# Units 8 to 31 of an attention kernel: two engines' queues in the order in which the program is written, with the pieces of a unit regrouped

## The chip, the cores and the metric

The kernel runs on one core of a Trainium2 chip. A core has a matrix engine (TensorE, PE in the rows; its weight loads are listed apart as PEld), a vector engine (VectorE, DVE), a scalar engine (ScalarE, ACT), a general engine (GpSimd, POOL) and a queue for transfers (SyncE, SP). Each engine works off its own queue in order and waits for others at semaphores. The metric is the device time of one execution in microseconds (us).

## The reference

Attention over 4 batches, 8 heads, 576 positions and 64 dimensions a head, followed by a two-layer network with a squared ReLU. To the scores of each head a bias is added that depends on the query's and the key's position alone; a small network of 32 hidden values makes it:

```
scores = scale * np.matmul(q, k.transpose(0, 1, 3, 2))
x = (psi_rel / psi_i)[..., None]
bias = np.maximum(x @ w1 + b1, 0.0) @ w2
scores = scores + bias.transpose(2, 0, 1)[None, :, :, :]
attn = softmax(scores)
out = np.matmul(attn, v)
h = np.maximum(out_as_tokens @ w_in, 0.0)
result = (h * h) @ w_out
```

## The kernel before

**Units.** A unit is one pair of heads of one batch and one chunk of 128 query positions (chunk 4 is the tail with 64 positions, in which the two heads share one tile). Units 0 to 39 (`NA` = 40) treat batches 0 and 1, eight units a chunk (`AB * HP` = 8), the tail's chunk first. While the eight units of one chunk run, the bias of the next chunk is made in 18 blocks of 32 key positions; units 0 to 31 make bias, units 32 to 39 have none left to make. Units from 40 on, and the two-layer network behind them, belong to other parts of the program, which the change does not touch.

**What a unit does.** The names are those of the rows:

- `sp` (L421): four score products into a PSUM tile of four banks, of which there is one.
- `t` (L431): VectorE adds the bias to a head's scores and finds the largest; twice a unit, once a head. `negm` is the largest.
- `p` (L436): ScalarE's exponential, twice a unit. The two are called the first and the second exponential here.
- `pp`, `pa` (L524, L516): TensorE transposes the probabilities of the unit two before (`TL` = 2): `pp` is four pieces of one head, so there are two of them a unit, the first and the second `pp`; `pa` is the last piece of both heads. ScalarE copies each to `pt` (L827).
- `bb` (L381): the masked products of a block, sixteen matrix products on a 0/1 mask that VectorE makes (`mask`, L371). ScalarE scales one half of a block (`bt`, L386); behind that, VectorE multiplies the other half (`bt`, L387); GpSimd adds them into the bias (`area`, L395). The mask tiles are three (`MB` = 3).
- `px` (L542): the products with the values, of a unit whose `pt` is there; VectorE copies the result (`xT`, L555; in the first eight units ScalarE does, L553).

**Blocks of a unit.** `BO` gives the number of blocks that are done by the end of each of the eight units of a chunk; from it units 8 to 15 have 1, 2, 3, 2, 3, 2, 3 and 2 blocks, as have 16 to 23; units 24 to 31 have 1, 2, 3, 2, 3, 2, 3 and 0.

**Banks.** The results `pp`, `pa`, `bb` and `px` go to four PSUM banks which one pool hands out in turn (`bank`, tag `aux`, four buffers). A result that comes fourth after another takes that one's bank, and TensorE's first product into it waits until the earlier result has been read out.

**Order.** The loop is written unit by unit: scores, exponentials, bias blocks, transposes, values. For units 0 to 39 a scheduler sorts each engine's queue by a simulated time of readiness; `keep_in_program_order` pins single instructions. Behind unit 39 the blocks `with tc.manual_schedule()` keep every queue in the order of the program text.

Of the kernel before, what the change touches and what calls it, by code (L numbers as in the profile page):

```python
# [22 lines left out]
HP = H // 2  # L23
# [4 lines left out]
AB = 2  # L28
NF = DFF // 128
NIC = 5  # L30
TAIL = 4
NJB = S // 32
# [6 lines left out]
BO, B1 = (3, 5, 8, 10, 13, 15, 18, 20), (12, 3, 8)  # L39
# [23 lines left out]
MB = 3  # L63
# [5 lines left out]
TL = 2  # L69
# [8 lines left out]
def attention_then_relu2_mlp(ctx: ExitStack, tc: tile.TileContext, q, k, v, cols, w_in, w_out, psi, xmat, dist, out):  # L78
# [64 lines left out]
    NA = len(units)  # L143
# [215 lines left out]
    def bias_mask(ic, jb):  # L359
        m = prep.tile([128, 8, 128], F16, name="mask", tag="mask", bufs=MB)  # L360
        if ic < TAIL:
            base = sdist[:, 128 * ic + 548 - 32 * jb:]
            win = bass.AP(tensor=base.tensor, offset=base.offset, ap=[base.ap[0], [4, 8], [1, 128]])
            th = theta[:, 128 * ic:128 * ic + 128].unsqueeze(1).to_broadcast([128, 8, 128])
            out = m
        else:
            base = sdist[:, 128 * ic + 548 - 32 * jb - HALF:]
            win = bass.AP(tensor=base.tensor, offset=base.offset, ap=[base.ap[0], [4, 8], [HALF, 2], [1, 64]])
            th = theta[:, 512:].unsqueeze(1).unsqueeze(1).to_broadcast([128, 8, 2, 64])
            out = m.rearrange("p g (x i) -> p g x i", x=2)  # L370
        DVE.tensor_tensor(out=out, in0=win, in1=th, op=ALU.is_ge)  # L371
        mask_t[ic, jb] = m

    def bias_sum(ic, jb):
        m = mask_t.pop((ic, jb))
        bb = bank("bb")
        t = prep.tile([128, H, 32], F32, name="bt1", tag="bt1", bufs=BB)
        s = prep.tile([128, H, 32], F32, name="bt2", tag="bt2", bufs=BB)
        for r in range(8):
            for n in range(2):  # L380
                PE.matmul(bb[:, 64 * (7 - r):64 * (8 - r)], lhsT=m[:, r], rhs=wmov[:, n], start=(n == 0), stop=(n == 1))  # L381
        xv = xc_t[ic][:, 32 * jb:32 * jb + 32].rearrange("p (g j) -> p g j", j=4).unsqueeze(1)
        bv = bb.rearrange("p (g a h j) -> p a h g j", g=8, a=2, h=H)
        tv = t.rearrange("p h (g j) -> p h g j", j=4)
        sv = s.rearrange("p h (g j) -> p h g j", j=4)
        ACT.activation(out=sv, in_=bv[:, 1], func=AF.Identity, scale=bscale)  # L386
        DVE.tensor_tensor(out=tv, in0=bv[:, 0], in1=xv.to_broadcast([128, H, 8, 4]), op=ALU.mult)  # L387
        if ic == TAIL:
            (POOL if jb < 7 else DVE).tensor_tensor(out=tail_sum[:, :, 32 * jb:32 * jb + 32], in0=t, in1=s, op=ALU.add)
            return  # L390
        dst = bias_t[:, 2 * ic, 32 * jb:]
        odd = S + (64 if jb < 16 else -512)
        dst = bass.AP(tensor=dst.tensor, offset=dst.offset, ap=[dst.ap[0], [9 * S, HP], [odd, 2], [1, 32]])
        tw, sw = (y.rearrange("p (e h) j -> p h e j", e=2) for y in (t, s))
        POOL.tensor_tensor(out=dst, in0=tw, in1=sw, op=ALU.add)  # L395
# [8 lines left out]
    def score_products(u, pin=True):  # L404
        b, hp, ic = units[u]
        kt, qt = k1_t[b, hp], q_t[b, hp]
        negm = att.tile([128, 2], F32, name="negm", tag="negm", bufs=3)
        if (b, hp) not in sum_t:
            sum_t[b, hp] = att.tile([128, 9], F32, name="sums", tag="sums", bufs=AB * HP + 2)
        p_t[u] = att.tile([128, 2 * S], F32, name="p", tag="p", bufs=PB)  # L410

        nsp = 2 if ic < TAIL else 1
        sp4 = ps.tile([128, 4, 512], F32, name="sp", tag="sp", bufs=1)
        sps = [sp4[:, 2 * n:2 * n + 2] for n in range(nsp)]
        cols = slice(128 * ic, 128 * ic + 128 if ic < TAIL else S)

        for m, (x, h) in enumerate((x, h) for x in range(2) for h in (1, 0)):
            rows = slice(64 * h, 64 * h + 64)
            k0 = HALF * x + (64 if h and ic == TAIL else 0)
            out_t, to = (sps[h], slice(0, 128)) if ic < TAIL else (sps[0], rows)  # L420
            mm = PE.matmul(out_t[to, x, :HALF], lhsT=qt[rows, cols], rhs=kt[rows, k0:k0 + HALF], start=True, stop=True)  # L421
            if m and pin:
                tc.keep_in_program_order(mm)
        return negm, sps

    def softmax(u, n, negm, sp):
        b, hp, ic = units[u]
        p, sums = p_t[u], sum_t[b, hp]
        bias = bias_t[:, 9 * hp + 2 * ic + n]
        t = att.tile([128, S], F32, name="t", tag="t", bufs=TB)  # L430
        DVE.tensor_tensor_reduce(  # L431
            out=t.rearrange("p (x n) -> p x n", x=2), in0=sp[:, :, :HALF],
            in1=bias.rearrange("p (x n) -> p x n", x=2), scale=-0.125, scalar=3.0e38,
            op0=ALU.add, op1=ALU.min, accum_out=negm[:, n:n + 1],
        )
        ACT.activation(out=p[:, S * n:S * n + S], in_=t, func=AF.Exp, bias=negm[:, n:n + 1], scale=-1.0, accum_out=sums[:, 2 * ic + n:2 * ic + n + 1])  # L436
        if ic == TAIL:
            POOL.tensor_copy(out=p[:, S:S + 64], in_=p[:, S - 64:S])
# [3 lines left out]
    def scores(u):  # L442
        negm, sps = begun.pop(u) if u in begun else score_products(u)
        for n, sp in enumerate(sps):
            softmax(u, n, negm, sp)
# [47 lines left out]
    def scale_x(b, hp, rows_t):  # L493
        times_rows(b, hp, *spread_rows(rows_t))

    def transposes(us, tags=None):
        next_tag = iter(tags) if tags else None
        groups = []
        pa = None
        for m, u in enumerate(us):  # L500
            p_of = p_t.pop(u)
            pt = att.tile([128, 9, 128], F32, name="pt", tag="pt", bufs=2)
            pt_t[u] = pt
            for h in range(2 if units[u][2] < TAIL else 1):
                groups.append((p_of, pt, h))
            groups.append((p_of, pt, None, m))
        if len(us) > 1:
            heads = [g for g in groups if g[2] is not None]
            groups = heads[:3] + [g for g in groups if g[2] is None] + heads[3:]
        last = []  # L510
        for p, pt, h, *m in groups:
            if h is None:
                if pa is None:
                    pa = bank("pa", "d" if tags and len(us) > 1 else next(next_tag) if tags else None)
                at = slice(128 * m[0], 128 * m[0] + 128)
                PE.transpose(pa[:, at], p[:, S - 64:S + 64], ident)  # L516
                last.append((pt[:, 8], pa[:, at]))
                if len(last) == len(us):
                    yield from last
            else:  # L520
                pp = bank("pp", next(next_tag) if tags else None)
                for c in range(4):
                    k0 = h * (S + 64) + 128 * c
                    PE.transpose(pp[:, 128 * c:128 * c + 128], p[:, k0:k0 + 128], ident)  # L524
                yield pt[:, 4 * h:4 * h + 4], pp.rearrange("p (c m) -> p c m", c=4)
# [54 lines left out]
            PE.matmul(warm[:, :128], lhsT=ones, rhs=ones, start=True, stop=True)  # L580

    todo = [(ic, jb) for ic in range(TAIL) for jb in range(NJB)]
    done = 0

    def bias_upto(n):
        nonlocal done
        while done < min(n, len(todo)):
            if done + 1 < len(todo):
                bias_mask(*todo[done + 1])
            bias_sum(*todo[done])  # L590
            done += 1

    with tc.manual_schedule():
        late, main = theta_steps(512, S), theta_steps(0, 512)[:2] + theta_steps(0, 128)[2:]
# [215 lines left out]
        return ic == (chunks[-1] if u < NA else NIC - 1)  # L810

    rest = theta_steps(128, 512)[2:]
    for s in range(NA):
        loads(s)
        scores(s)
        if s and rest:
            tc.keep_in_program_order(rest.pop(0)())
        if s < AB * HP * TAIL:
            n, r = divmod(s, AB * HP)
            if r == 7 and n + 2 < NIC:  # L820
                tc.keep_in_program_order(scale_xc(chunks[n + 2]))
            bias_upto(NJB * n + BO[r])
            if r == 1 and n + 2 < NIC:
                load_xc(chunks[n + 2])
        if s >= TL:
            for dst, src in transposes((s - TL,)):
                ACT.copy(dst, src)  # L827
        u = s - TL - 1
        if u >= 0:
            for piece in values((u,)):  # L830
                keep_values(*piece)
            b, hp, ic = units[u]
            if ends(u):
                waiting.append((b, hp, normalise(b, hp)))
            if waiting and waiting[0][:2] != (b, hp):
                scale_x(*waiting.pop(0))

    prep_stack.close()
    half_stack.close()
# [482 lines left out]
```

## Time and profile before

| | us |
|---|---|
| median of 3 runs | 724.46 |
| lowest, highest | 724.44, 724.8 |
| the profiled execution, its own time | 724.39 |
| its span in the profile | 722.6 |
| TensorE busy in the span | 691.2 |
| VectorE busy | 554.6 |
| ScalarE busy | 474.8 |
| GpSimd busy | 186.6 |

The profile is of one execution. A row of the timeline is a group of equal instructions: its start counted from the span's start, how long it lasts, engine, line, operation, what is written and read, shapes, count, and in brackets how long its engine had been idle before it and what ended that. TensorE's weight loads (PEld) come ahead of their matrix products, so their starts tell where TensorE's queue stands; the ends of matrix products are modelled by the profiler.

### The profile page before, as it was taken

To read this page: it belongs to the slowest core of one execution; us is meant where nothing else is said; L and a number is where in the kernel's file an instruction comes from. 1 tells how busy PE (TensorE), PEld (TensorE's weight loads), DVE (VectorE), ACT (ScalarE), POOL (GpSimd) and SP (SyncE) were. 2 spreads that over 40 slices of the span, in tenths; PEclk is the share of its full clock that TensorE was granted. 3 is DMA by queue.
4 is the path that set the end of the run, shared out by engine and by line. 5 is a ranking of instruction groups with operands and counts; after the bars stand their busy time and mean duration, and the time that the engine had idled before them with its cause. 6 is when DMAs were issued, how large, how long until landed. Compare 5 with 4: busy or idle time off the path is not lost.

```text
span 722.6 us, 17384 instructions
## 1 busy us (share of the span) xinstructions
PE 691.2 (96%) x6966; PEld 565.0 (78%) x6966; DVE 554.6 (77%) x1165; ACT 474.8 (66%) x954; POOL 186.6 (26%) x313
## 2 busy tenths in 40 slices
PE   7799999999999999899999999999999999999992
PEld 6577777787777877678878888888888888888881
DVE  8998888775588999889898969777468875566761
ACT  5678778777587888798666766666465564454220
POOL 6563433331110156444332304112011111000000
PEclk9999999999999999999999999999999999999997
DMA  6640000004449521410613333050067303533100
GB/s 187 200 123 3 19 2 2 3 2 118 169 162 286 163 85 36 136 60 14 236 59 161 147 160 117 8 212 1 1 201 294 134 14 134 187 117 117 59 2 29
DMA packets 31620, 75.13 MB, mean 104 GB/s; under 512 B 5556, under 2 KB 13876, under 8 KB 30516
## 3 DMA queue, kind: packets, MB, share of 16 engines
q1 hardware_dynamic: 31540, 74.03, 30.5%
q8 instruction: 55, 0.90, 0.5%
q14 instruction: 25, 0.20, 0.1%
HBM read 55.66 MB, written 18.35 MB: 102 GB/s over the span
## 4 chain that ended last, share of the span: by engine, by line
PE 79%; DVE 12%; ACT 4%; issue 2%; DMA 1%; ACTq 0%; DVEq 0%
PE y L1198 26%; PE ha L1103 12%; PE sp L421 9%; PE px L542 9%; PE hb L1103 9%; PE pp L524 8%; PE bb L381 4%; DVE t L431 2%; DVE mask L371 2%; ACT pt L1041 1%; PE pa L516 1%; ACT p L436 1%; DVE bt L387 1%; DMA raw<-in_w_in 1%; DVE wa L198 1%
## 5 line engine op out<-in xcount | busy, mean ns | idle before, releaser
L1103 PEld LDWEIGHTS <-area 128*128 128x128 f16 x1680 | 147.7, 98 | 25.1 <-issue 8.4
L1198 PE MATMUL y<-w,gh 128*128 128x512 f32 x576 | 149.1, 398 | 1.2 <-ACT gh L1142 1.2
L431 DVE CUSTOM_DVE_ANT_0 t<-sp,area 128x576 f32<-128x576 f32 x144 | 104.3, 752 | 26.0 <-PE sp L421 16.6
L1198 PEld LDWEIGHTS y<-w,gh 128*128 128x128 f32 x576 | 105.0, 188 | 23.4 <-ACT gh L1142 2.2
L436 ACT ACTIVATE p<-t,negm 128x576 f32<-128x576 f32 x144 | 111.9, 787 | 12.5 <-DVE negm L431 11.8
L421 PE MATMUL sp<-k,q 64*128 64x288 f32 (+1 forms) x640 | 98.5, 425 | 4.0 <-DVE negm L431 3.2
L542 PE MATMUL px<-pt,v 128*64 128x128 f32 (+1 forms) x1600 | 92.2, 266 | 1.6 <-DVE xT L491 0.8
L542 PEld LDWEIGHTS px<-pt,v 128*64 128x64 f32 x1600 | 79.2, 137 | 17.6 <-ACT pt L1041 7.1
L1103 PE MATMUL ha<-area 128*128 128x256 f16 (+1 forms) x816 | 84.8, 260 | 0.3 <-DVE c L1120 0.3
L524 PE MATMUL pp<-ident,p 128*128 128x128 f32 x576 | 78.9, 277 | 2.9 <-DVE xT L491 1.7
L1198 PE MATMUL y<-w,gl 128*128 128x512 f32 x288 | 79.0, 390 | 0.0
L395 POOL TENSOR_TENSOR area<-bt,bt 128x256 f32<-128x256 f32 x72 | 53.6, 767 | 78.5 <-DVE bt L387 78.5
L524 PEld LDWEIGHTS pp<-ident,p 128*128 128x128 f32 x576 | 62.2, 141 | 13.2 <-issue 7.5
L421 PEld LDWEIGHTS sp<-k,q 64*128 64x128 f32 (+1 forms) x640 | 53.3, 175 | 24.3 <-issue 5.7
L1103 PE MATMUL hb<-area 128*128 128x256 f16 (+1 forms) x612 | 65.0, 260 | 0.0
L1198 PEld LDWEIGHTS y<-w,gl 128*128 128x128 f32 x288 | 54.1, 188 | 12.2 <-DVE gl L1143 0.2
L371 DVE TENSOR_TENSOR mask<-sdist,theta 128x1024 f16<-128x1024 f16 x81 | 55.8, 726 | 5.6 <-PE bb L381 5.2
L381 PEld LDWEIGHTS <-mask 128*128 128x128 f16 x1296 | 42.3, 100 | 12.2 <-DVE mask L371 6.8
L381 PE MATMUL bb<-wmov,mask 128*128 128x64 f16 x1296 | 47.4, 196 | 4.4 <-DVE mask L371 4.1
L1041 ACT COPY pt<-pp 128x512 f32<-128x512 f32 x76 | 41.1, 602 | 15.2 <-PE pp L524 15.1
L827 ACT COPY pt<-pp 128x512 f32<-128x512 f32 x68 | 37.7, 588 | 14.4 <-PE pp L524 14.4
L1143 DVE TENSOR_TENSOR gl<-area,gh 128x512 fp32r<-128x512 f32 (+1 forms) x40 | 25.4, 668 | 26.3 <-ACT gh L1142 24.2
(164 smaller groups left out, 987.7 us busy)
## 6 DMA issues: line engine op xcount, KB each, us to landing
raw<-in_w_in SPq DMA_DIRECT2D x32, 512.0 KB, 4.5
r<-in_w_out SPq DMA_DIRECT2D x16, 512.0 KB, 5.5
xs<-area SPq DMA_DIRECT2D x4, 1792.0 KB, 11.9
py<-o SPq DMA_DIRECT2D x12, 512.0 KB, 2.7
o<-py SPq DMA_DIRECT2D x12, 512.0 KB, 4.4
v<-in_v SPq DMA_DIRECT2D x16, 320.0 KB, 4.2
q<-in_q SPq DMA_DIRECT2D x32, 128.0 KB, 3.0
out<-o SPq DMA_DIRECT2D x8, 512.0 KB, 2.9
```

Source lines behind the costliest of these rows:

```text
L371: DVE.tensor_tensor(out=out, in0=win, in1=th, op=ALU.is_ge)
L381: PE.matmul(bb[:, 64 * (7 - r):64 * (8 - r)], lhsT=m[:, r], rhs=wmov[:, n], start=(n == 0), stop=(n == 1))
L395: POOL.tensor_tensor(out=dst, in0=tw, in1=sw, op=ALU.add)
L421: mm = PE.matmul(out_t[to, x, :HALF], lhsT=qt[rows, cols], rhs=kt[rows, k0:k0 + HALF], start=True, stop=True)
L431: DVE.tensor_tensor_reduce(out=t.rearrange("p (x n) -> p x n", x=2), in0=sp[:, :, :HALF], in1=bias.rearrange("p (x n) -> p x n", x=2), sca ...
L436: ACT.activation(out=p[:, S * n:S * n + S], in_=t, func=AF.Exp, bias=negm[:, n:n + 1], scale=-1.0, accum_out=sums[:, 2 * ic + n:2 * ic + n ...
L524: PE.transpose(pp[:, 128 * c:128 * c + 128], p[:, k0:k0 + 128], ident)
L542: PE.matmul(px[64 * h:64 * h + 64, 128 * m:128 * m + w], lhsT=vt[:, c, h], rhs=src, start=(c == 0), stop=(c == 4))
L827: ACT.copy(dst, src)
L1041: ACT.copy(*c)
L1103: PE.matmul(h[:, s, :w], lhsT=a, rhs=x, start=(k == 0), stop=(k == 5))
L1198: PE.matmul(y_t[n][k], lhsT=(gl if m == 2 else gh)[:, slot, o:o + 128], rhs=wl if m == 1 else wh, start=((n, P) in firsts and f == 0 and m ...
```

## The change

For units 8 to 31 the queues of TensorE and VectorE keep the order of the program text; ScalarE, GpSimd and SyncE are still sorted by the scheduler. The text of such a unit is now: scores, exponentials, the two `pp` and `pa` of the unit two before, the masked products of the unit's blocks, the values of the unit three before. Masks are made three blocks ahead: the mask of a later block is made between a block's scaling on ScalarE and its multiplication on VectorE. Units 0 to 7 and 32 to 39 keep the scheduler's order.

```
-    def bias_sum(ic, jb):
+    def bias_sum(ic, jb, then=None):
...
         ACT.activation(out=sv, in_=bv[:, 1], func=AF.Identity, scale=bscale)
+        if then:
+            then()
         DVE.tensor_tensor(out=tv, in0=bv[:, 0], in1=xv.to_broadcast([128, H, 8, 4]), op=ALU.mult)
...
+    def step(s, plain=True):
         loads(s)
-        scores(s)
+        if plain:
+            scores(s)
+        else:
+            negm, sps = score_products(s, False)
+            for n, sp in enumerate(sps):
+                softmax(s, n, negm, sp)
...
+        def turned():
+            for dst, src in transposes((s - TL,)):
+                ACT.copy(dst, src)
+
+        if not plain:
+            turned()
+        if n < TAIL:
...
+            if plain:
+                bias_upto(NJB * n + BO[r])
+                if s == AB * HP - 1:
+                    mask_upto(done + MB)
+            else:
+                sum_upto(NJB * n + BO[r], lambda: mask_upto(done + MB + 1))
...
+        if plain and s >= TL:
+            turned()
...
+    for s in range(AB * HP):
+        step(s)
+    with tc.manual_schedule(engines={PE.engine, DVE.engine}):
+        for s in range(AB * HP, NA - AB * HP):
+            step(s, False)
+    for s in range(NA - AB * HP, NA):
+        step(s)
```

TensorE's queue in unit 20, which has three blocks, before (the sixteen products of a block are shown by their first; the number in a name tells one tile from another):

```order
L421 MATMUL sp_2312<-k1_465,q1_468 128x288 x4
L516 MATMUL pa_2295<-ident_81,p_2018 128x128
L542 MATMUL px_2298<-pt_2193,v_107 64x128 x10
L381 MATMUL bb_2325<-wmov_93,mask_2258 128x64
...
L381 MATMUL bb_2349<-wmov_93,mask_2323 128x64
...
L381 MATMUL bb_2373<-wmov_93,mask_2347 128x64
...
L524 MATMUL pp_2396<-ident_81,p_2109 128x128 x4
L421 MATMUL sp_2425<-k1_475,q1_478 128x288 x4
```

And the same unit of the change:

```order
L423 MATMUL sp_2318<-k1_465,q1_468 128x288 x4
L526 MATMUL pp_2330<-ident_81,p_2115 128x128 x4
L526 MATMUL pp_2336<-ident_81,p_2115 128x128 x4
L518 MATMUL pa_2342<-ident_81,p_2115 128x128
L381 MATMUL bb_2345<-wmov_93,mask_2211 128x64
...
L381 MATMUL bb_2369<-wmov_93,mask_2276 128x64
...
L381 MATMUL bb_2393<-wmov_93,mask_2300 128x64
...
L544 MATMUL px_2417<-pt_2240,v_439 64x128 x10
L423 MATMUL sp_2431<-k1_475,q1_478 128x288 x4
```

The transposes, which stood partly ahead of the scores, now all stand between the scores and the blocks, and the values have moved from ahead of the blocks to behind them; the transposes are of unit 18 instead of 17 and 18.

ScalarE's queue from the first exponential of unit 20 to that of unit 21, before:

```order
L436 ACTIVATE p_2311,sums_823<-t_2317,negm_2310 128x576
L436 ACTIVATE p_2311,sums_823<-t_2320,negm_2310 128x576
L386 ACTIVATE bt2_2327<-bb_2325,small_89 128x256
L386 ACTIVATE bt2_2351<-bb_2349,small_89 128x256
L386 ACTIVATE bt2_2375<-bb_2373,small_89 128x256
L827 COPY pt_2395<-pp_2396 128x512
L827 COPY pt_2395<-pp_2402 128x512
L827 COPY pt_2395<-pa_2408 128x128
L436 ACTIVATE p_2424,sums_930<-t_2430,negm_2423 128x576
```

And of the change:

```order
L438 ACTIVATE p_2317,sums_823<-t_2323,negm_2316 128x576
L838 COPY pt_2329<-pp_2336 128x512
L838 COPY pt_2329<-pa_2342 128x128
L386 ACTIVATE bt2_2347<-bb_2345,small_89 128x256
L438 ACTIVATE p_2317,sums_823<-t_2326,negm_2316 128x576
L386 ACTIVATE bt2_2371<-bb_2369,small_89 128x256
L386 ACTIVATE bt2_2395<-bb_2393,small_89 128x256
L838 COPY pt_2442<-pp_2443 128x512
L438 ACTIVATE p_2430,sums_930<-t_2436,negm_2429 128x576
```

The copy of the first `pp` of a unit (`pp_2443` of unit 21) stands ahead of that unit's first exponential, and the copies of the second `pp` and of `pa` (`pp_2336`, `pa_2342` of unit 20) stand behind it; before, the three copies stood together.

## Rows read from the trace of the kernel before

**Rows 1.** The page: span, busy time of each engine

```profile
span 722.6 us, 17384 instructions
...
PE 691.2 (96%) x6966; PEld 565.0 (78%) x6966; DVE 554.6 (77%) x1165; ACT 474.8 (66%) x954; POOL 186.6 (26%) x313
```

**Rows 2.** Windows: length, busy (count) of PE, PEld, DVE, ACT, POOL; clock, DMA, GB/s

```profile
52.08:66.99 14.91, 14.74 (x264) 11.61 (x264) 13.54 (x34) 13.23 (x38) 5.96 (x9) 1.00 0.02 7
66.99:86.84 19.85, 19.85 (x314) 15.94 (x313) 16.98 (x41) 15.94 (x43) 7.43 (x10) 1.00 0.07 18
86.84:124.72 37.88, 37.88 (x585) 30.20 (x585) 31.31 (x77) 29.90 (x76) 12.69 (x18) 1.00 0.01 2
124.72:157.54 32.82, 32.82 (x512) 26.13 (x511) 26.05 (x66) 26.01 (x67) 10.61 (x16) 1.00 0.01 2
157.54:161.79 4.25, 4.25 (x44) 3.26 (x43) 2.37 (x7) 3.08 (x9) 2.06 (x3) 1.00 0.02 4
161.79:199.58 37.79, 36.74 (x408) 28.27 (x407) 20.84 (x67) 25.72 (x67) 5.51 (x29) 1.00 0.44 137
```

**Rows 3.** Waits of PE from 24 to 200 us: the longest; us, times, longest one

```profile
PE pp L524 <- DVE bt L387: 1.0, 2, 0.8
```

**Rows 4.** Timeline, unit 20, which has three blocks

```profile
105.31 0.79 PEld L421 LDWEIGHTS sp<-k,q 64*128 64x128 f32 x8 [0.17 <-issue]
...
106.48 0.14 PEld L516 LDWEIGHTS pa<-ident,p 128*128 128x128 f32 x1 [0.39 <-ACT pt L827]
...
106.60 0.76 DVE L431 CUSTOM_DVE_ANT_0 t<-sp,area 128x576 f32<-128x576 f32 x1 [0.59 <-PE sp L421]
106.74 1.07 PEld L542 LDWEIGHTS px<-pt,v 128*64 128x64 f32 x20
...
107.40 0.78 ACT L436 ACTIVATE p<-t,negm 128x576 f32<-128x576 f32 x1 [0.29 <-DVE negm L431]
...
107.98 1.46 PEld L381 LDWEIGHTS <-mask 128*128 128x128 f16 x48 [0.17 <-issue]
...
108.10 0.29 DVE L555 COPY xT<-px 128x128 f32<-128x128 f32 x1
...
108.66 1.90 DVE L371 TENSOR_TENSOR mask<-sdist,theta 128x1024 f16<-128x1024 f16 x3 [0.27 <-PE bb L381]
```

**Rows 5.** Timeline, unit 21, which has two blocks

```profile
111.13 0.42 PEld L524 LDWEIGHTS pp<-ident,p 128*128 128x128 f32 x4 [0.39 <-issue]
...
111.52 0.14 PEld L516 LDWEIGHTS pa<-ident,p 128*128 128x128 f32 x1
...
111.83 0.58 ACT L827 COPY pt<-pp 128x512 f32<-128x512 f32 x1 [1.17 <-PE pp L524]
...
112.31 0.27 ACT L827 COPY pt<-pa 128x128 f32<-128x128 f32 x1
112.46 0.79 ACT L436 ACTIVATE p<-t,negm 128x576 f32<-128x576 f32 x1
...
113.23 0.77 ACT L436 ACTIVATE p<-t,negm 128x576 f32<-128x576 f32 x1
...
113.99 0.86 PEld L524 LDWEIGHTS pp<-ident,p 128*128 128x128 f32 x8
113.99 0.84 ACT L386 ACTIVATE bt<-bb,small 128x256 f32<-128x256 f32 x2
...
114.96 0.41 DVE L387 TENSOR_TENSOR bt<-bb,xc 128x256 f32<-128x256 f32 x1
```

**Rows 6.** Timeline, unit 6: a wait of TensorE that a copy of ScalarE ends

```profile
44.98 0.57 ACT L827 COPY pt<-pp 128x512 f32<-128x512 f32 x1
...
45.60 0.20 PEld L542 LDWEIGHTS px<-pt,v 128*64 128x64 f32 x4 [0.69 <-ACT pt L827]
```

**Rows 7.** Timeline, end of unit 8: from values to scores

```profile
55.17 0.66 PEld L542 LDWEIGHTS px<-pt,v 128*64 128x64 f32 x20 [0.17 <-ACT p L436]
...
55.90 0.79 PEld L421 LDWEIGHTS sp<-k,q 64*128 64x128 f32 x8
```

More of the change, by code (lines that the diff above doesn't have):

```diff
@@ L582, in attention_then_relu2_mlp, with mask_upto, sum_upto, bias_upto @@
     todo = [(ic, jb) for ic in range(TAIL) for jb in range(NJB)]
-    done = 0
-    def bias_upto(n):
+    done, made = 0, 1
+    def mask_upto(n):
+        nonlocal made
+        while made < min(n, len(todo)):
+            bias_mask(*todo[made])
+            made += 1
+    def sum_upto(n, then=None):
         nonlocal done
         while done < min(n, len(todo)):
-            if done + 1 < len(todo):
-                bias_mask(*todo[done + 1])
-            bias_sum(*todo[done])
+            bias_sum(*todo[done], then)
             done += 1
+    def bias_upto(n):
+        while done < min(n, len(todo)):
+            mask_upto(done + 2)
+            sum_upto(done + 1)
     with tc.manual_schedule():
@@ L812, in attention_then_relu2_mlp @@
     rest = theta_steps(128, 512)[2:]
-    for s in range(NA):
+    def step(s, plain=True):
         loads(s)
-        scores(s)
+        if plain:
[4 more added lines that the diff above has]
+                softmax(s, n, negm, sp)
         if s and rest:
             tc.keep_in_program_order(rest.pop(0)())
-        if s < AB * HP * TAIL:
-            n, r = divmod(s, AB * HP)
+        n, r = divmod(s, AB * HP)
+        def turned():
[4 more added lines that the diff above has]
+        if n < TAIL:
             if r == 7 and n + 2 < NIC:
                 tc.keep_in_program_order(scale_xc(chunks[n + 2]))
-            bias_upto(NJB * n + BO[r])
+            if plain:
[4 more added lines that the diff above has]
+                sum_upto(NJB * n + BO[r], lambda: mask_upto(done + MB + 1))
             if r == 1 and n + 2 < NIC:
                 load_xc(chunks[n + 2])
-        if s >= TL:
-            for dst, src in transposes((s - TL,)):
-                ACT.copy(dst, src)
+        if plain and s >= TL:
+            turned()
         u = s - TL - 1
```

## Prediction

> **What bounds the kernel now.** I read the page first [rows 1]: TensorE is busy for 691.2 of 722.6 us, VectorE for 554.6, ScalarE for 474.8. An average says little about one stage, so next I cut the stretch of the changed units into windows at the starts of the scores [rows 2]: units 8 to 11, 12 to 15, 16 to 23, 24 to 30, 31, and 32 to 40 behind them. From unit 12 to 31 TensorE is busy for the whole of each window, and the four windows last 19.85, 37.88, 32.82 and 4.25 us. The granted clock is 1.00 in all of them. The list of TensorE's waits says the same: between 24 and 200 us its longest entry is 1.0 us in two times [rows 3], and the same view of 86.84 to 161.79 us has no entry. So in these units nothing but TensorE's own queue sets the pace; a piece of work saved there counts in full, and so does any wait put there.
>
> Then I read two units row by row. In the weight loads one sees gaps at which TensorE waits for nobody [rows 4, 5]: 0.39 us behind the scores, 0.17 ahead of them, 0.17 between the values and the blocks, and 0.12 or 0.17 between `pa` and the values (106.74 less 106.62; 111.83 less 111.66). They stand where the rows change from one shape of tile (64*128, 128*128, 128*64) to another. Between `pp`, `pa` and blocks, all 128*128, there is none to speak of.
>
> **What the change removes and adds on TensorE.** No product is added or taken away. All 128*128 work of a unit now stands together, so a unit has three changes of shape for four. Scores to `pp` stays 0.39. Blocks to values isn't in the trace: between 0 and the 0.17 of `pa` to values; I take 0.07, what a group with 64 columns shows ahead of the scores [rows 7]. Values to scores with 128 columns isn't there either: between that 0.07 and the 0.39 behind the scores; I take 0.17, since the same values show it ahead of blocks [rows 4]. The Trainium skill, "TensorEngine Tiling (Array Packing)", section Tiling Modes, says that changing the tiling mode drains TensorE; the gaps of rows 4 and 5 agree, and by that rule alone the change is a gain, the first rival below.
>
> Without any wait a unit would last: scores and their gap 1.17 (105.31 to 106.48), two `pp` 0.86 and `pa` 0.14, blocks 0.49 each (1.46 for three, 0.99 for two), 0.07, values 1.07, 0.17 [rows 4, 5]. That is 4.94 us with three blocks, 4.47 with two, 3.97 with one.
>
> **The wait that comes instead.** The four banks go round in turn, so in the new order the bank of each result is plain to count. In a unit the fourth result behind the first `pp` is the second block, and the fourth behind the second `pp` is the third block where there are three, or the values where there are two. So the third block, or the values, must wait until ScalarE has copied the second `pp` of the same unit. In the order before, the copy asked for had been issued about a unit earlier. And ScalarE's new queue puts the second `pp`'s copy behind the unit's first exponential, which needs the scores just computed. I follow this chain from the start of a unit's scores:
>
> - the first `pp` starts at 1.17; its copy can start 0.70 after (111.13 to 111.83), at 1.87, and takes a slot of 0.48 (111.83 to 112.31): 2.35 [rows 5];
> - VectorE's `t` starts at 1.29 (105.31 to 106.60), the first exponential could at 2.09 (107.40) [rows 4]; it stands behind that copy, so 2.35, and takes a slot of 0.77 (112.46 to 113.23): 3.12 [rows 5];
> - the second `pp`'s copy lasts 0.58: 3.70 [rows 5]; TensorE goes on 0.05 later (45.55 to 45.60) [rows 6]: 3.75.
>
> The third block would have started at 1.17 + 1.00 + 0.97 = 3.14 and so waits 0.61; the values of a two-block unit at 3.23 and wait 0.52. What is queued behind them is the next unit's scores, and with them everything. A three-block unit lasts 3.75 + 0.49 + 0.07 + 1.07 + 0.17 = 5.55, a two-block unit 3.75 + 1.07 + 0.17 = 4.99. This can't drift apart over the units, since the chain starts anew at each unit's scores. With one block the values take the bank of the first `pp`, copied by 1.87 + 0.58 = 2.45, before they need it: 3.97. Unit 31 has no block, and its values find their bank free.
>
> **The sum.** By windows [rows 2]:
>
> - units 12 to 15 (3, 2, 3, 2 blocks): 21.08 for 19.85, +1.23;
> - 16 to 23 (one of one block, four of two, three of three): 3.97 + 19.96 + 16.65 = 40.58 for 37.88, +2.70;
> - 24 to 30: 3.97 + 14.97 + 16.65 = 35.59 for 32.82, +2.77;
> - 31: 1.17 + 1.00 + 0.17 + 1.07 + 0.17 + 0.42 + 0.17 = 4.17 for 4.25, with half the next transposes, -0.08;
> - 8 to 11, where tail units pass with half the values (0.66 [rows 7]) and one `pp`: 3.75 + 3.52 + 5.04 + 4.99 = 17.30 for 14.91, +2.39. In unit 10 the chain holds too.
>
> Together +9.01. But the values now run three units behind the scores, where the queue before ran four behind from unit 9 on. At unit 32 the change is one set of values and one `pp` ahead: 1.07 + 0.17 + 0.42 = 1.66 us that units 32 to 40 needn't do. I take it as given back in full, since TensorE is busy for 36.74 of 37.79 us there; if the waits of that stretch swallow it, nothing comes back. Net +7.35: 724.39 + 7.35 = **731.7 us**. The profiled execution's 724.39 (span 722.6 and 1.8 around it) is 0.07 below the median, so no correction.
>
> **What costs nothing.** Masks three ahead: TensorE isn't waiting for masks in these units, so it gains nothing; a mask made at the third block before has more than a unit's time as cover, and would cost only if VectorE fell that far behind. VectorE's multiplications now stand one by one behind ScalarE's scalings. In a three-block unit ScalarE goes on at 3.60 with `pa` (0.15), scaling (0.42), second exponential (0.77) and two scalings: 4.17, 5.36 and 5.78 are their ends [rows 5]. VectorE follows with 0.41 a multiplication [rows 5] and 0.63 a mask [rows 4]: 4.58, 5.77 and, behind the third mask at 6.40, 6.81; the copy of the values (0.29 [rows 4]) ends at 7.10. The next `t` is due at 5.55 + 1.29 = 6.84 and is 0.26 late. Its exponential would be at 2.09 + 0.26 = 2.35, just when the copy ahead of it ends: free, with no slack left. SyncE's and GpSimd's queues keep their order, and the transfers for unit 40 on are issued from unit 34, later with the rest.
>
> **Rivals.**
>
> 1. *The gaps saved count and no wait comes.* It needs the second `pp` copied by 3.14, that is ScalarE to reach it without the exponential between, or other banks than I count. Then the windows are 16.17, 18.82, 36.67, 32.20 and 4.17: -1.68, and with the 1.66 ahead -3.34: 721.0 us. For it: a saturated TensorE and the gaps in the rows. Against it: ScalarE's order in the change. This is the side on which the change is faster. Chance 0.08.
> 2. *VectorE decides as well.* The chain of scalings and multiplications has no slack at 0.26. I counted no hand-over time in it; with six hand-overs at the 0.05 of rows 6 up to twice that, each of the nine three-block units from 10 to 30 delays its successor's exponential by 0.3 to 0.6: 2.7 to 5.4 us more, 734.4 to 737.1. For it: VectorE has 31.31 us of work in 37.88 [rows 2], in a stricter order. Against it: hand-overs may overlap with masks. Chance 0.15.
> 3. *The wait is there but made up for.* If ScalarE overlaps the first copy with the exponential (2.09 for 2.35), every unit of two or three blocks is 0.26 shorter, 18 units or so: 4.7 less, 727.0; only with the gaps at their low ends (0.07 less for blocks to values, 0.10 less for values to scores, 20 units: 3.4 less) does it come near 724. Against it: ScalarE's rows stand one behind the other. Chance 0.07.
>
> The forecast, 0.70. Its own range: gaps at their low ends 728.3, at the high end of values to scores (0.22 more, 20 units) 736.1, the 1.66 not given back 733.4.
>
> **The numbers.** A difference of 0.2%, 1.4 us, is about what a measurement can tell from none. The forecast, rival 2 and half of rival 3 are slower than that: 0.88; rival 1 is faster: 0.08; the rest of rival 3 is no change: 0.04. For 8 in 10 the range leaves out rival 1 and the far end of 3, and takes in rival 2: 727.5 to 738.
>
> **What would show it.** Right: in TensorE's waits a new entry of some 0.5 to 0.6 us, 16 to 20 times, from ScalarE's `pt` copy to `bb` and `px`; starts of scores 4.99 and 5.55 us apart in turn between units 12 and 30, and 3.97 in units 16 and 24; scalar rows in the order copy, exponential, copy; no 0.17 between values and blocks. Wrong: units of 4.47 and 4.94 us without such waits (rival 1); a wait of the scores or of `t` for VectorE's multiplications (rival 2); units 32 to 40 as long as before, 37.79 us (nothing given back). A span behind unit 40 that changes by more than a microsecond would put the cause outside this account.

## The result, and the profile after

The change takes 731.18 us (median of 5 runs, 731.02 to 731.68) where the kernel before, run beside it, took 724.44 (median of 5, 724.17 to 724.80): a ratio of 1.0095, with a 95% interval of 1.0080 to 1.0109. The profiled execution took 731.02 us, its span is 729.2. The forecast was 731.7, slower, within 727.5 to 738.

The page of the change, its span and the busy times:

```profile
span 729.2 us, 17379 instructions
...
PE 688.8 (94%) x6966; PEld 566.4 (78%) x6966; DVE 555.5 (76%) x1165; ACT 473.7 (65%) x954; POOL 197.9 (27%) x313
```

TensorE is busy for 2.4 us less than before [rows 1], with as many products (6966), in a span that is 6.6 longer: there is more waiting, not more work. The windows of the change, cut at the same units as [rows 2] (units 8 to 11, 12 to 15, 16 to 23, 24 to 30, 31, and 32 to 40), with the same columns:

```profile
51.90:69.42 17.52, 16.51 (x290) 13.69 (x289) 14.31 (x35) 14.87 (x43) 7.36 (x10) 1.00 0.02 7
69.42:90.48 21.06, 19.31 (x311) 16.12 (x309) 16.18 (x40) 14.69 (x39) 9.28 (x10) 1.00 0.07 17
90.48:131.17 40.69, 37.52 (x586) 31.23 (x584) 31.60 (x77) 29.36 (x76) 16.82 (x18) 1.00 0.01 2
131.17:166.89 35.72, 32.99 (x518) 27.48 (x516) 26.82 (x66) 26.06 (x68) 14.63 (x16) 1.00 0.01 2
166.89:171.02 4.13, 4.13 (x43) 3.14 (x41) 2.57 (x8) 2.44 (x7) 1.41 (x2) 1.00 0.02 4
171.02:206.41 35.39, 35.04 (x384) 26.84 (x383) 20.57 (x66) 25.09 (x66) 5.55 (x29) 1.00 0.46 146
```

From unit 12 to 30 TensorE was busy for the whole of each window before; now it is idle for 1.75, 3.17 and 2.73 us of three of them. The granted clock is 1.00 here as there, so the clock has no part in it. Units 8 to 31 last 119.12 us for 109.71, +9.41; units 32 to 40 last 35.39 for 37.79, -2.40; unit 8 begins 0.18 earlier (51.90 for 52.08), and what lies behind unit 40 is 0.23 shorter (522.79 for 523.02). Together +6.60, the difference of the spans.

TensorE's waits between 52 and 200 us, where [rows 3] had nothing above 1.0 us in two times (us in total, times, longest one):

```profile
PE px L544 <- ACT pt L838: 4.6, 10, 0.5
PE bb L381 <- ACT pt L838: 4.1, 9, 0.5
PE sp L423 <- DVE negm L433: 0.4, 1, 0.4
```

Nine three-block units and ten two-block units stand between unit 10 and unit 30, and the two new entries count nine and ten. Where they sit shows in the timeline of units 20 and 21, whose scores start at 110.12 and 115.66:

```profile
110.12 0.79 PEld L423 LDWEIGHTS sp<-k,q 64*128 64x128 f32 x8 [0.17 <-issue]
...
111.29 0.85 PEld L526 LDWEIGHTS pp<-ident,p 128*128 128x128 f32 x8 [0.39 <-issue]
...
111.98 0.59 ACT L838 COPY pt<-pp 128x512 f32<-128x512 f32 x1 [1.49 <-PE pp L526]
...
112.46 0.78 ACT L438 ACTIVATE p<-t,negm 128x576 f32<-128x576 f32 x1
...
113.23 0.57 ACT L838 COPY pt<-pp 128x512 f32<-128x512 f32 x1
...
113.86 0.63 PE L381 MATMUL bb<-wmov,mask 128*128 128x64 f16 x16 [0.44 <-ACT pt L838]
113.86 0.50 PEld L381 LDWEIGHTS <-mask 128*128 128x128 f16 x15 [0.53 <-issue]
...
115.66 0.79 PEld L423 LDWEIGHTS sp<-k,q 64*128 64x128 f32 x8 [0.17 <-issue]
...
117.00 0.74 DVE L433 CUSTOM_DVE_ANT_0 t<-sp,area 128x576 f32<-128x576 f32 x1
...
119.40 1.07 PEld L544 LDWEIGHTS px<-pt,v 128*64 128x64 f32 x20 [0.56 <-ACT pt L838]
...
120.64 0.79 PEld L423 LDWEIGHTS sp<-k,q 64*128 64x128 f32 x8 [0.17 <-issue]
```

ScalarE's rows stand as copy, exponential, copy: the second copy begins at 113.23, 3.11 behind the scores, because an exponential of 0.78 stands ahead of it, and ends at 113.80. TensorE goes on with the third block at 113.86. In unit 21, which has two blocks, it is the values that wait, 0.56, of which 0.05 is the change of shape that stands there without a wait too.

### The profile page after: what moved, and what is told of

Its sections match the earlier page's. It is cut to its first block, busy times and chain, and to the rows that moved or that the text cites. A ratio compares the mean times of both kernels' runs of the same rounds, so it can differ in the third digit from the quotient of the medians.

```text
span 729.2 us, 17379 instructions
## 1 busy us (share of the span) xinstructions
PE 688.8 (94%) x6966; PEld 566.4 (78%) x6966; DVE 555.5 (76%) x1165; ACT 473.7 (65%) x954; POOL 197.9 (27%) x313
## 4 chain that ended last, share of the span: by engine, by line
PE 77%; DVE 11%; ACT 8%; issue 3%; DMA 0%; ACTq 0%; DVEq 0%
PE y L1233 26%; PE ha L1138 12%; PE sp L423 10%; PE px L544 10%; PE hb L1138 9%; PE pp L526 7%; ACT pt L838 3%; ACT p L438 3%; DVE t L433 2%; DVE mask L371 2%; PE bb L381 2%; ACT pt L1076 1%; DVE bt L389 1%; PE pa L518 1%; DVE wa L198 1%
## 5 line engine op out<-in xcount | busy, mean ns | idle before, releaser
L397 POOL TENSOR_TENSOR area<-bt,bt 128x256 f32<-128x256 f32 x72 | 64.4, 906 | 77.0 <-DVE bt L389 76.7
L526 PE MATMUL pp<-ident,p 128*128 128x128 f32 x576 | 77.4, 277 | 2.6 <-DVE xT L493 1.7
L371 DVE TENSOR_TENSOR mask<-sdist,theta 128x1024 f16<-128x1024 f16 x81 | 58.1, 727 | 3.0 <-PE bb L381 0.6
L389 DVE TENSOR_TENSOR bt<-bb,xc 128x256 f32<-128x256 f32 x81 | 33.4, 419 | 20.8 <-ACT bt L386 19.1
```

## The experiments

Each kernel is the change with one or two edits. The kernel before was run beside them on the same chip: 724.43, 724.21 and 724.16 us (medians of 14, 13 and 13 runs) in three sittings, the first four kernels in the first, the next three in the second, the last two in the third.

**The copies ahead of the exponentials (e1).** ScalarE's queue is held in the written order too, and a unit's exponentials are written behind its three copies (part 1 of `softmax` is VectorE's addition, part 2 the exponential).

```
-                softmax(s, n, negm, sp)
+                softmax(s, n, negm, sp, 1)
...
+            for m, sp in enumerate(sps):
+                softmax(s, m, negm, sp, 2)
...
-    with tc.manual_schedule(engines={PE.engine, DVE.engine}):
+    with tc.manual_schedule(engines={PE.engine, DVE.engine, ACT.engine}):
```

> Units 8 to 31 with ScalarE's queue in written order as well, and the unit's two exponentials written behind the three copies of pp, pp, pa. Nothing is left out. Theory (the wait for the bank of the second pp, whose copy stands behind the first exponential): that copy now ends about 2.9 us after the start of the scores and no block or set of values waits for it, so the 19 entries of some 0.46 us for ScalarE's pt copy are gone. But VectorE's multiplications now stand behind both exponentials, each mask behind a multiplication, and its loop (t, two exponentials, scaling, multiplications and masks, copy of the values) takes about 10.0 us for a pair of units of three and two blocks, against 10.53 in the change and 9.41 if TensorE alone decided: about 726.5 us, in a range of 721 to 728. Rival (the stricter queues of TensorE and VectorE cost the time, not ScalarE's order): 731 as the change.

Measured: 727.01 us (726.73 to 727.36), ratio to before 1.0037 (1.0024 to 1.0050). Both waits for the `pt` copy are gone, and a three-block unit lasts 4.95, its length without a wait. But TensorE now waits at another place. TensorE's waits in this kernel, 52 to 200 us:

```profile
PE pa L525 <- DVE bt L389: 3.1, 9, 0.4
PE bb L381 <- DVE bt L389: 0.8, 2, 0.6
```

`pa` is the fourth result behind the last block of the unit ahead and takes its bank. In the seven two-block units from 13 to 29 that follow a three-block unit, and in units 16 and 24, it waits until VectorE has multiplied that block; the two-block units that wait last 5.08 to 5.15, units 17 and 25, which don't, 4.48. This is the rival in which VectorE decides; it comes to light once the exponential is out of the way. Part of the lateness is of this edit's making, since ScalarE's scalings now stand behind both exponentials: the third block of unit 20 is multiplied 7.11 us behind the start of the unit's scores (115.58 less 108.47), in the change 6.35 (116.47 less 110.12).

**The same, and the masks of a unit ahead of its multiplications (e2).** On VectorE the blocks' multiplications now stand side by side, behind all masks of the unit.

```
-        if then:
-            then()
+        if then is not None:
+            mask_upto(done + MB + 1)
+            then.append(lambda: finish(ic, jb, t, s, tv, bv, xv))
+            return
...
-                sum_upto(NJB * n + BO[r], lambda: mask_upto(done + MB + 1))
+                late = []
+                sum_upto(NJB * n + BO[r], late)
+                for fn in late:
+                    fn()
```

`finish` holds the multiplication and the adds behind it.

> As the kernel with the copies first, and on VectorE a unit's masks stand ahead of its multiplications instead of one by one between them. Nothing is left out. Theory: VectorE's masks fill the time in which ScalarE does the exponentials, its queue ends ahead of the next unit's t within 0.3 us, and TensorE waits for nobody: units of 4.94 and 4.47 us, 10 x 0.52 + 9 x 0.61 = 10.7 us less than the change, 720.5 us, under both kernels. Rival (the queue in written order costs by itself): at or above 726.

Measured: 720.58 us (720.44 to 721.62), ratio to before 0.9951 (0.9936 to 0.9966): faster than both kernels. The one wait listed between 52 and 200 us is of 0.3 us, ahead of the scores of unit 39. The windows of units 12 to 15 and 16 to 23:

```profile
68.32:87.17 18.85, 18.85 (x310) 15.99 (x308) 16.46 (x40) 14.69 (x40) 7.06 (x10) 1.00 0.06 18
87.17:124.02 36.85, 36.85 (x586) 31.02 (x584) 30.78 (x76) 29.34 (x77) 12.74 (x18) 1.00 0.01 2
```

TensorE is busy throughout both, and for 1.00 and 1.03 us less than before [rows 2]. Units 20 and 21 of this kernel:

```profile
105.17 0.79 PEld L428 LDWEIGHTS sp<-k,q 64*128 64x128 f32 x8 [0.17 <-issue]
...
107.04 1.07 ACT L850 COPY pt<-pp 128x512 f32<-128x512 f32 x2 [0.99 <-PE pp L538]
...
108.16 0.80 ACT L438 ACTIVATE p<-t,negm 128x576 f32<-128x576 f32 x1
...
110.12 0.79 PEld L428 LDWEIGHTS sp<-k,q 64*128 64x128 f32 x8 [0.17 <-DVE mask L371]
...
110.20 1.16 DVE L394 TENSOR_TENSOR bt<-bb,xc 128x256 f32<-128x256 f32 x3 [0.25 <-ACT bt L386]
...
114.60 0.19 PEld L428 LDWEIGHTS sp<-k,q 64*128 64x128 f32 x2 [0.17 <-issue]
```

Both copies end by 108.11, 2.94 behind the scores, just ahead of the 3.14 at which the third block wants its bank; the units last 4.95 and 4.48, where the prediction had 4.94 and 4.47 for units without a wait.

**`pa` ahead of the two `pp` (e3).** The queues stay as in the change; only the three transposed pieces change places, so that each result's bank moves on by one.

```
+        if front:
+            groups = [g for g in groups if g[2] is None] + [g for g in groups if g[2] is not None]
...
-            for dst, src in transposes((s - TL,)):
+            for dst, src in transposes((s - TL,), None, not plain):
```

> The change with one thing moved: pa is transposed ahead of the two pp, so the banks shift by one; ScalarE's queue is still the scheduler's. Nothing is left out. Theory: the fourth result behind the second pp is now the values in a unit of three blocks and the next unit's first transpose in a unit of two; the third block and the values of two-block units wait only for the first pp's copy, which is early. Two-block units 4.47; in three-block units the values wait some 0.2 to 0.4 us: 5.15 to 5.3. 10 x 0.52 + 9 x 0.26 = 7.5 us less than the change: 723.7 us (722 to 725.5). Rival (VectorE's order decides): 731, as the change.

Measured: 722.96 us (722.51 to 724.05, 10 runs), ratio 0.9980 (0.9971 to 0.9990). In the timeline of unit 20, whose scores start at 105.97, the exponential still stands between the copies:

```profile
107.95 0.59 ACT L840 COPY pt<-pp 128x512 f32<-128x512 f32 x1 [0.17 <-PE pp L528]
...
108.43 0.78 ACT L438 ACTIVATE p<-t,negm 128x576 f32<-128x576 f32 x1
...
109.20 0.57 ACT L840 COPY pt<-pp 128x512 f32<-128x512 f32 x1
...
109.83 1.07 PEld L546 LDWEIGHTS px<-pt,v 128*64 128x64 f32 x20 [0.20 <-ACT pt L840]
```

The second copy begins even later in the unit than in the change (3.23 behind the scores for 3.11), yet TensorE stands for only 0.20 ahead of the values, and some of that (0.05 in units without a wait) is the change of shape: the result that asks for that bank is now the values, one block later, and in two-block units it falls into the next unit. Three-block units last 5.10, two-block units 4.48. So the late copy is not the cost by itself; which result asks for its bank is.

**The values ahead of the blocks (e4).** `valued()` holds the lines of the values, which move up:

```
+        if not plain:
+            valued()
...
+        if plain:
+            valued()
```

> The change with the values written ahead of the masked products instead of behind them (and VectorE's copy of them ahead of the masks). Nothing is left out. Theory: the same ScalarE order, but the blocks, which take the banks of the two pp and pa, come 1.2 us later in the unit, when the copies are done; so the wait goes, and the fourth change of tile shape comes back (0.17 behind pa, 0.17 behind the values, 0.07 ahead of the scores). Units near those before, 5.1 to 5.3 and 4.65 to 4.8 us, a pair 9.8 to 10.1: 724 to 727 us. Rival (queues in written order cost by themselves): 731.

Measured: 728.61 us (728.26 to 728.68), ratio 1.0058 (1.0041 to 1.0074): above what was expected. Three-block units last 5.05 and wait for nothing, but two-block units behind a three-block one last 4.90 to 5.07 (units 17 and 25, behind a one-block unit, 4.59). The timeline of unit 21, whose scores start at 114.14, from the second of the multiplications of unit 20's blocks to its own values:

```profile
115.31 0.42 DVE L389 TENSOR_TENSOR bt<-bb,xc 128x256 f32<-128x256 f32 x1
115.65 0.89 DVE L371 TENSOR_TENSOR mask<-sdist,theta 128x1024 f16<-128x1024 f16 x1
...
116.46 0.41 DVE L389 TENSOR_TENSOR bt<-bb,xc 128x256 f32<-128x256 f32 x1
...
116.93 1.07 PEld L544 LDWEIGHTS px<-pt,v 128*64 128x64 f32 x20 [0.66 <-DVE bt L389]
```

The values are the fourth result behind the third block of the unit ahead, and VectorE multiplies that block only behind a mask of 0.89. It is the lateness of VectorE that e1 showed, at another bank; that the mask takes 0.89 and not the 0.68 of the one ahead of it has to do with GpSimd's adds (last section).

**The values ahead of the blocks, and the masks ahead of the multiplications (e8).** The edits of e4 and, on VectorE, of e2, to test that reading.

> Values ahead of the blocks as in the run before (728.61), and all masks of a unit ahead of its multiplications on VectorE. There the values of a two-block unit waited for VectorE's multiplication of the last block of the unit ahead (bank counting: that block is the fourth result before them); units of two blocks lasted 4.90 to 5.07 where unit 17, without a wait, lasted 4.59. Theory (late VectorE holds the bank): with multiplications side by side behind the last scaling the waits go, 0.17 to 0.79 us in each of eleven units, 4.7 together: 728.6 - 4.7 = 723.9, with 0.8 us in unit 40 that may come or go: 722.8 to 724.7. Rival (the wait is for something else, as ScalarE's copies): 728 to 729, with the values still waiting in two-block units.

Measured: 725.17 us (724.71 to 725.55, 10 runs), ratio 1.0011 (1.0001 to 1.0020). The values' waits for VectorE are gone, 3.4 us of 4.7 come back, and 725.17 lies 0.5 above the range given. Seven of the two-block units last 4.72 and not the 4.59 of unit 17, 0.91 together, and unit 10 lasts 4.98 and not 4.54 (its 4.71 in e4 less the wait there), 0.44 more: 723.9 + 0.91 + 0.44 = 725.25. The rows of unit 21, and the entry for unit 10 in TensorE's waits from 52 to 210 us, show what these rests are:

```profile
116.12 1.12 PEld L381 LDWEIGHTS <-mask 128*128 128x128 f16 x32 [0.17 <-issue]
116.12 0.57 ACT L843 COPY pt<-pp 128x512 f32<-128x512 f32 x1
```

```profile
PE bb L381 <- ACT pt L843: 0.3, 1, 0.3
```

In this order the second block comes fourth behind the second `pp`. The copy of that `pp` in unit 21 ends at 116.69, and the second block's loads go on at 116.74, 0.13 late, so that the two blocks take 1.12 for the 0.99 of unit 17; in unit 10 the copy ends at 63.84 and the second block goes on at 63.89. All eight units show it in their single loads. VectorE's wait is gone, as the theory says, and what is left is the change's own wait, shorter.

**The masks ahead of the multiplications alone (e9).** The edit of e2 on VectorE, ScalarE's order as in the change.

> The change with one edit: all masks of a unit ahead of its multiplications on VectorE, ScalarE's order as in the change. Theory (what bounds the changed units is the second pp's copy behind the first exponential, VectorE is hidden): no change, 731.2 (730.4 to 732.0), units of 5.54 and 4.99 with the same waits for the pt copy. Rival (VectorE's lateness decides, as it did where the copies came first, 6.4 us): 725 to 728.

Measured: 732.05 us (732.03 to 732.06), ratio 1.0108 (1.0091 to 1.0125). TensorE's waits, 52 to 210 us:

```profile
PE px L549 <- ACT pt L843: 4.5, 10, 0.5
PE bb L381 <- ACT pt L843: 4.1, 9, 0.5
PE px L549 <- DVE xT L498: 0.8, 1, 0.8
```

Units of 5.54 and 4.99, waits as in the change. An edit that was worth 6.4 us between e1 and e2 is worth nothing here: while ScalarE's copy ends last, VectorE's order is hidden. The time lies 0.05 above the range; the 0.9 us above the change is for the most part the third row, a wait in unit 40, of which more below.

**TensorE's queue alone in the written order (e6).**

```
-    with tc.manual_schedule(engines={PE.engine, DVE.engine}):
+    with tc.manual_schedule(engines={PE.engine}):
```

> The change with TensorE's queue alone in written order; VectorE's is left to the scheduler again. Nothing is left out. Theory (the wait is one of TensorE for ScalarE): the same waits and the same periods of 4.99 and 5.54 us, 731 us within 0.5. Rival (VectorE's strict order takes part): less than 729.

Measured: 731.93 us (731.76 to 732.15), ratio 1.0107 (1.0092 to 1.0123). The same units and waits (4.5 us in 10 times, 4.1 in 9), and the wait of unit 40, by which the time lies 0.4 above the range given. The whole loss comes with TensorE's order; VectorE's has no part in it.

**`pa` ahead, and the masks ahead (e7).** The edits of e3 and, on VectorE, of e2.

> pa transposed ahead of the two pp, and VectorE's masks of a unit ahead of its multiplications; ScalarE's queue is the scheduler's. Nothing is left out. Theory: as with pa first alone, but VectorE is no longer late at the next unit's t, so the first exponential and with it the second pp's copy come earlier: the values of a three-block unit wait 0.2 us instead of 0.35; units of 5.13 and 4.47 us: 722.2 us (721 to 723.5). If VectorE's lateness has no part in it, the same as with pa first alone.

Measured: 723.56 us (723.04 to 724.95, 10 runs), ratio 0.9992 (0.9983 to 1.0001), 0.60 above e3 where 0.8 below was expected. Units 20 and 21 last 5.10 and 4.48, as in e3, so the 0.20 left there is not VectorE's but the copy's; a wait in unit 40 of 0.8, which this kernel has (the unit lasts 8.27) and e3 has not (7.50), is enough for the 0.60 above it.

**Masks made one block ahead (e5).** The masks as in the kernel before, on the change.

```
-                if s == AB * HP - 1:
-                    mask_upto(done + MB)
             else:
-                sum_upto(NJB * n + BO[r], lambda: mask_upto(done + MB + 1))
+                bias_upto(NJB * n + BO[r])
```

> The change with masks made as before, each one block ahead and ahead of the block's own multiplication, in the same order of text otherwise. Nothing is left out. Theory: in written order the mask of the second block stands behind both t of the unit (ready at about 3.4 us after the start of the scores), that of the third behind the first multiplication (5.2 us): the second block waits for VectorE in two-block units (5.25 us a unit), the third in three-block units (7.1). 9 x 1.5 + 10 x 0.26 = 16 us more than the change: 747 us (742 to 751), TensorE's waits naming VectorE's mask. Rival (masks ahead are worth nothing, as TensorE didn't wait for masks before): 731.

Measured: 758.75 us (755.20 to 760.91), ratio 1.0467 (1.0431 to 1.0502): the direction is as expected, the size was too small by 12. The longest of TensorE's waits, 52 to 200 us:

```profile
PE bb L381 <- ACT bt L386: 12.0, 9, 1.4
PE bb L381 <- DVE mask L371: 11.0, 19, 1.1
```

These are the second block's wait in units of two or three blocks and the third's, both for a mask (the first row names ScalarE, but the load of the mask in unit 20 names the mask, below). Windows of unit 20 and the beginning of unit 21 (scores at 123.90 and 132.23), cut where TensorE's pace changes; the granted clock is the third number from the end:

```profile
127.30:128.50 1.20, 0.64 (x16) 0.52 (x16) 0.33 (x1) 1.20 (x4) 0.00 (x0) 1.00 0.00 0
128.50:129.90 1.40, 0.65 (x16) 0.56 (x16) 1.31 (x4) 0.76 (x3) 1.22 (x2) 0.92 0.00 0
129.90:132.20 2.30, 2.30 (x22) 2.00 (x20) 0.86 (x2) 0.47 (x1) 1.75 (x2) 0.50 0.03 7
...
133.40:134.90 1.50, 1.50 (x15) 1.10 (x14) 0.98 (x3) 0.40 (x1) 0.00 (x0) 1.00 0.00 0
```

The waits are what was expected: in units 8 to 31 TensorE is idle for 24.29 us (147.08 less 122.79 busy), in the change for 8.66 (119.12 less 110.46), and the difference is 15.6. The rest, 12.3 us, is in the busy time, and most of it is the clock: behind two pauses the granted clock is at 0.50 for the values of unit 20, and at 1.00 again from 133.40. The mean granted clock is 0.88, 0.90 and 0.96 in the windows of units 12 to 15, 16 to 23 and 24 to 30, which last 27.84, 51.87 and 42.71; what is missing to 1.00 comes to 10.2 us, the most that the clock can have cost. At least 2 us come from elsewhere: units 8 to 11 are busy for 16.97 us at a clock of 1.00, in the change for 16.51, and unit 28 for 5.29, where unit 20 of the change is busy for 5.10. What makes them was not looked into.

## Why the prediction was right

**The gaps at changes of shape: right.** 0.39 from scores to `pp` (111.29) and 0.17 from values to scores (115.66) are as taken; from blocks to values it is 0.05 (e2: 108.83 to 108.88) for the 0.07 taken. The trace before showed the last two in other pairs only; in e2 units without a wait last 4.95 and 4.48 for 4.94 and 4.47 worked out. The Trainium skill, "TensorEngine Tiling (Array Packing)", section Tiling Modes, says that a change of mode drains TensorE; the rows agree, with 0.39, 0.17 and 0.05 us at the three changes of a unit. What it is worth here shows in e2, where no wait stands in the way: units 8 to 31 last 108.50 us for 109.71, with 1.63 us of work in them that the kernel before does later, 2.84 saved for the 3.34 of the first rival.

**The chain of the wait: right to 0.02 us.** Behind the scores of unit 20 (110.12) the prediction had the first copy at 1.87, the exponential at 2.35, the second copy from 3.12 to 3.70 and TensorE at 3.75; the rows have 1.86, 2.34, 3.11, 3.68 and 3.74. Unit 20 lasts 5.54 for 5.55, unit 21 4.99 for 4.99, and e1 takes both waits away by moving the exponential. That the bank's turn is the link, and not ScalarE's work, is shown by e3, where the copy comes as late and TensorE waits 0.20 for 0.53.

**The sum: 0.4 short in the units.** Units 12 to 15 last 21.06 for 21.08, 16 to 23 40.69 for 40.58, 24 to 30 35.72 for 35.59, unit 31 4.13 for 4.17, and 8 to 11 17.52 for 17.30. The units behind a one-block unit are 0.05 longer than the rest of their kind (5.04 and 5.60), four times; that and 0.22 in the first four units make most of the difference between +9.41 and +9.01. Units 16 and 24, with one block, last 4.02 and 4.01 for 3.97.

**What units 32 to 40 give back: 2.40 for 1.66, and the difference is another thing.** In the kernel before, the second set of values in unit 40 waits once for VectorE; the change lacks that wait. It stands in TensorE's waits of the kernel before, 186 to 208 us:

```profile
PE px L542 <- DVE xT L491: 0.8, 1, 0.8
```

The weight loads of that set in e9, which has the wait too:

```profile
204.08 0.96 PEld L549 LDWEIGHTS px<-pt,v 128*64 128x64 f32 x18 [0.89 <-DVE xT L498]
```

And in the change:

```profile
203.06 1.07 PEld L544 LDWEIGHTS px<-pt,v 128*64 128x64 f32 x20
```

The wait lengthens unit 40 by 0.77 (8.27 in e7 for 7.50 in e3), so 1.63 of the 2.40 is the work done ahead, which was taken as 1.66. The prediction didn't see this wait. It is there in the one trace each of the kernel before, e4 and e6 to e9, and absent from the change, e1, e2, e3 and e5, and follows no edit that was made; why it comes and goes was not settled. Differences of 0.8 us between these kernels are read with that in mind.

**How near the total came is in part luck.** The forecast of +7.35 and the +6.60 of the spans differ by 0.75: the units were 0.40 longer than worked out, and against that stand the 0.77 of unit 40, of which nothing was known, and 0.41 ahead of unit 8 and behind unit 40, which were taken as unchanged. The kernels with the wait of unit 40 and otherwise the units of the change take 731.93 (e6) and 732.05 (e9).

**What was costed at nothing.** VectorE: hidden, as said, with more slack than was worked out. `t` of unit 21 begins 1.34 behind its scores (117.00), 0.05 later than VectorE could and not 0.26; e6 and e9 show no time in its order. Masks three ahead: they gain nothing against the kernel before, as said, but that was not free to leave out: in the new order masks one block ahead cost 27.6 us more than three (e5).

**The rivals.** That the gaps count and no wait comes needed the second copy by 3.14: e2 brings it to 2.94 and takes 720.58, for 721.0 worked out, the two closer than their parts, since e2 also lacks the wait of unit 40. The change itself doesn't meet the condition. That VectorE decides as well: no, since the copy hides it; e1 and e4 show that it is the next limit, in orders that also make VectorE later, with 3.9 us of waits in the one and 3.8 in the other. That the copy overlaps the exponential: no, the exponential begins 0.48 behind the copy (111.98 and 112.46), the slot that was taken.

## What to carry to other kernels

When products are regrouped on a saturated engine, count for every result how many others lie between it and the next user of its buffer, and follow the reader of that buffer through its own queue: here a reader that stood behind one exponential cost 10.6 us in units 8 to 31 (119.12 for the 108.50 of e2), where the regrouping saved 2.84, and moving the results by one bank (e3: 110.85) gave 8.3 of it back. An order on two engines is tuned together with that of the third; remove the last wait and look for the next one before judging an edit, since the masks' order was worth 0 us behind one wait (e9) and 6.4 us once that was gone (e2).

## What the hardware showed that was not expected

**The clock fell after short pauses.** In e5 TensorE paused for 0.67 us ahead of the second block of unit 20 and for 1.43 ahead of the third, with 0.52 of loads between them. Its weight loads of the second and third block and of the values:

```profile
127.30 0.52 PEld L381 LDWEIGHTS <-mask 128*128 128x128 f16 x16 [0.67 <-DVE mask L371]
...
129.25 0.56 PEld L381 LDWEIGHTS <-mask 128*128 128x128 f16 x16 [1.43 <-DVE mask L371]
129.90 2.00 PEld L544 LDWEIGHTS px<-pt,v 128*64 128x64 f32 x20
```

The twenty loads of the values took 2.00 us where unit 20 of the change takes 1.07: the granted clock of 0.50 is the lower of the two levels, 1.2 GHz for 2.4, and it was 1.00 again by 133.40. Of the nine three-block units behind unit 9 six had such a fall and last 8.2 to 8.7 us. The same two pauses in units 28 and 30 (both 7.16 long, with 5.3 of busy time) were followed by no fall, and the pauses of the change, 0.5 once a unit, left the clock at 1.00. In e5 15.6 us of further pauses brought up to 10.2 us of slower work with them. Its four runs go with the mean clock of each: 755.20 us at 0.987, 757.78 at 0.981, 759.73 at 0.980, 760.91 at 0.977. What tells the units with a fall from those without was not tried.

**A GpSimd add and a VectorE mask that run side by side can both take longer.** The adds of the change from 69 to 155 us (count, then shortest, median and longest in ns):

```profile
L397 POOL TENSOR_TENSOR area<-bt,bt x38: 721/1102/1126, 69.2 to 151.7; 128x256 f32<-128x256 f32 x38
```

And of e2:

```profile
L402 POOL TENSOR_TENSOR area<-bt,bt x43: 724/732/745, 69.4 to 153.2; 128x256 f32<-128x256 f32 x43
```

The adds of the change are of two kinds. Compared one by one with VectorE's masks, 21 of the 38 have a mask running for 0.5 to 0.7 us of their time and last 1.10 to 1.13 us; the other 17 have none and last 0.72 to 0.74. In this stretch of all eleven traces each add beside a mask takes 1.10 us or more and each other at most 0.75. In e9, which differs from the change in VectorE's order alone, no add meets a mask and the mean is 0.73 for 0.94, so the masks' place is the cause; how the one holds up the other is not shown. In the change it cost no time: no wait of TensorE or VectorE between 52 and 200 us names an add. In e1 and e4 the masks take longer too: in each kernel, the seven masks in which an add begins 0.3 us after their own start last 0.88 to 0.89 us, all others 0.68 to 0.69. They stand ahead of the multiplication for which TensorE waits (in unit 21 of e4 the one at 115.65), so an estimated 0.2 us of each of these seven waits goes with the adds.
